# Sparse attention and two expert layers on one core: tiles moved to one offset modulo 512 bytes, scores in quadrants, the last tile's row operations issued later

## Chip, cores and metric

One core of one Trainium2 chip runs the whole program. The metric is the device time of one execution in microseconds (us). The kernel before takes 958.8 us (median of 3 runs, 957.45 to 959.18).

## What is computed

```python
# attention: q, k, v of 4 batches x 8 heads x 576 tokens x 64
scores = (1 / 8) * q @ k.T
scores = where(scores >= max(scores, -1) - tau, scores, -1e9)
attn = exp(scores - max(scores, -1))
attn = attn / (sum(attn, -1) + 1e-9)
x = attn @ v                        # then heads side by side: 2304 x 512
# first expert layer, d_ff 1536
y = ((x @ w_a) * (x @ w_b)) @ w_out
# second expert layer, d_ff 1024
h = y @ w_in
e = exp(h - max(h, -1))
s = h * e / (sum(e, -1) + 1e-9)
ln = (s - mean(s)) / sqrt(var(s) + 1e-6) * g_ln
out = ln @ w_out2
```

All is float32. In the expert layers each operand is split into a high part (rounded to fp32r) and the remainder, and a product is three matmuls: high x high, high x low, low x high.

## The kernel before

The work is issued in the order in which the code stands; each engine takes its instructions in that order.

**Attention** (`attention`) works on 16 pairs of heads (`i`). A pair has nine score tiles `s`: for each of four chunks of 128 tokens one per head, and a ninth, the tail, that holds the last 64 tokens of both heads. The loop over `m` takes two score tiles per step, so nine steps are two pairs. For a tile, `scores` (L281 to L289) multiplies queries by keys on TensorE. The 64-long inner dimension stands twice in the partitions: the lower 64 partitions (`g` = 0) multiply the first half of the keys, the upper 64 (`g` = 1) the second half, into two PSUM banks of one `ps` tile. A float32 matmul of the program runs in two passes and stands twice in the trace, with two weight loads. For a normal tile the products are of 64 rows by 128 columns of the array, for the tail of 64 by 64, with one head in each half of the columns. Then VectorE scales and takes the row minimum (L293, `ns`), ScalarE takes the exponential (L305, `pe`), GpSimd works out the threshold (L310), VectorE masks (L319). A step later TensorE transposes `pe` (L339, and L355, L358 for tails), ScalarE copies it to SBUF (L332), and two steps later TensorE multiplies with `v` (L370). `finish` transposes the reciprocals of a pair (L391, `rt`), ScalarE copies them (L396, `zt`), and a DMA stores them. `rt`, `tp` and `tq` share three PSUM buffers. `PROG` sets the order within a step.

**Weights** arrive as float64 bits; `conv_load` brings 512 columns at a time (`wraw`), and `conv_ops` makes float32 of them (L127 ACT, L131, L134, L137 DVE) and splits them (L141 ACT, L144 POOL). The results go to nine slots of 12288 bytes, five in pool `wp` (w1 groups with `f % 9 < 5`: w1_0 to w1_4 and w1_9 to w1_11, later w2_0 and w2_1) and four in pool `wp2` (w1_5 to w1_8, w2_2 to w2_5).

**First expert layer** (`moe1`): 12 groups `f` of 128 hidden columns, 5 blocks `j` of tokens, four of 512 columns and one of 256 (the tails of all batches). In a first pass every block goes through groups 0 to 5, in a second through 6 to 11. `ab` (L549) makes 24 matmuls, weights `w1_f` loaded and input `xt` streamed; ACT and DVE make `a`, `g` and `gt` (L555 to L558); two units later `yacc` (L572) makes 12 matmuls, weights `w1_f` and `gt` streamed.

**Second expert layer** (`moe2`): 18 tiles `t` of 128 tokens. `hid(t)` makes 24 matmuls (L656: `ys` loaded, `w2` streamed) and then issues the row operations: maximum (L660), exponential (L663), product (L664), mean (L666), centring (L667, `e`), sum of squares (L668), scale (L670 to L677). `lnt(t)` transposes `e` (L689, `pl`), multiplies by `g_ln` (L693, `l`), rounds (L694) and subtracts (L695, on GpSimd, for the last tile on VectorE) to make `lt`. `outp(t)` makes 24 matmuls (L708: `lt` loaded, `w2` streamed), ACT scales the result (L713), a DMA stores it. The loop issues `hid(t)`, `outp(t-2)`, `lnt(t-1)`; at the last tile, 17, `lnt(16)` comes between `hid(17)` and `outp(15)`, and after the loop come half of `outp(16)`, `lnt(17)`, the other half, and `outp(17)`.

Where tiles lie: pools follow each other in SBUF in the order in which they are opened. In the program as built, the pool `const` ends at byte 17184 of a partition, which is 288 modulo 512. The five slots of `wp`, the staging tiles (`wraw`, `w32`, `wlow`) and `xr0`, `zr` stand at 288 modulo 512. Then come the four `vs` tiles of 32 bytes, 128 bytes in all, and everything behind them that the expert layers use (`xt`, the four slots of `wp2`, `gt`, `a32`, `g32`, `ys`, `lt`, `y1`) stands at 416 modulo 512.

Of the kernel before, what the change touches and what calls it, by code (L numbers as in the profile page):

```python
# [8 lines left out]
F32 = mybir.dt.float32  # L9
# [5 lines left out]
ALU = mybir.AluOpType  # L15
AX = mybir.AxisListType
PSUM = bass.MemoryType.PSUM
P = 128
# [3 lines left out]
def kernel(  # L22
# [11 lines left out]
    nc = tc.nc  # L34
    NP, _, VS, D = v.shape
    NQ = VS // 2
    SM = NQ * P
    S = SM + D
    W = S + D
    NT, DM = out.shape  # L40
    B = NT // S
    NPAIR = NP // B
    NF = w1.shape[0]
    KC = DM // P
    DF2 = w_in.shape[2]
    NJ = DF2 // P
    HS = S // 2
# [8 lines left out]
    NTILE = len(TILES)  # L56
# [10 lines left out]
    const = ctx.enter_context(tc.tile_pool(name="const", bufs=1))  # L67
# [17 lines left out]
    xr_p = ctx.enter_context(tc.tile_pool(name="xr", bufs=1))  # L85
# [3 lines left out]
    vs = {}  # L89
# [92 lines left out]
    def load_x(j):  # L182
        n = LEN[j]
        xr = xr_p.tile([P, KC, NB], F32, name="xr0")[:, :, 0:n]
        zr = xr_p.tile([P, KC, NB], F32, name="zr")[:, :, 0:n]
        for b, s0, m, c in BLK[j]:
            nc.sync.dma_start(out=xr[:, :, c:c + m], in_=xd[b][:, :, s0:s0 + m])
            if b not in vs:
                vs[b] = xr_p.tile([P, KC, 2], F32, name="vs", bufs=B)
                nc.sync.dma_start(out=vs[b], in_=xd[b][:, :, S:S + 2])  # L190
                vnew.append(b)
            for h in range(2):
                zs = rzd[b].rearrange("(k h) s -> h k s", h=2)[h:h + 1, :, s0:s0 + m]
                nc.sync.dma_start(out=zr[h * D:(h + 1) * D, :, c:c + m], in_=zs.to_broadcast([D, KC, m]))
        xs[j] = (xr, zr, xhs[j % 2].tile([P, KC, 2, NB], F32R, name="xt")[:, :, :, 0:n])
# [40 lines left out]
    def attention():  # L236
# [43 lines left out]
        def scores(i, s):  # L280
            q, k = ld[i]  # L281
            ps = ps_s.tile([P, 2, 512], F32, name="ps")
            qc, h = divmod(s, 2)
            parts = [(slice(0, P), h, slice(qc * P, (qc + 1) * P), 0)] if s < 2 * NQ else [(slice(u * D, (u + 1) * D), u, slice(SM, S), u * D) for u in range(2)]
            for rows, u, c, o in parts:
                for g in range(2):
                    r = slice(g * D, (g + 1) * D)
                    nc.tensor.matmul(ps[rows, g, 0:HS], lhsT=q[r, u, c], rhs=k[r, u, o:o + HS], start=True, stop=True, skip_group_check=True)  # L288
            st[i, s] = ps  # L289

        def soft_max(i, s, nm):
# [113 lines left out]
        for h in range(2):  # L405
            nc.scalar.dma_start(out=q0[:, h], in_=qkv[0, :, h * (W + D):h * (W + D) + S])
            for g in range(2):
                r, o = slice(g * D, (g + 1) * D), (2 + h) * W + g * HS
# [21 lines left out]
        for m in range(tot // 2 + 6):  # L430
            if m == tot // 2 - 10:
                load_x(0)
# [58 lines left out]
            i, s = divmod(2 * m, NS)  # L491
            r = m - (i * NS + 1) // 2
# [145 lines left out]
    def moe2(ps_t):  # L638
# [5 lines left out]
        def w2(i, u):  # L644
            return w2s[i // 3][:, i % 3, u]

        s1 = {}

        def hid(t):
            y = yt.pop(t)  # L650
            ph = ps_s.tile([P, 2, 512], F32, name="ps")
            for g in range(2):
                k = 0
                for kc in range(KC):
                    for a, b in ((0, 0), (0, 1), (1, 0)):
                        nc.tensor.matmul(ph[:, g, :], lhsT=y[:, a, kc, :], rhs=w2(2 * kc + g, b), start=(k == 0), stop=(k == 3 * KC - 1))  # L656
                        k += 1
            nm = sm.tile([P, 1], F32, name="nm")
            z = sm.tile([P, 3], F32, name="z2")
            nc.vector.tensor_reduce(out=nm, in_=ph, axis=AX.XY, op=ALU.max, negate=True)  # L660
            e = wstage.tile([P, DF2], F32, name="e", tag="wraw", bufs=RB)
            ev = e.rearrange("p (g n) -> p g n", g=2)
            nc.scalar.activation(out=ev, in_=ph, func=AF.Exp, bias=nm, scale=1.0, accum_out=z[:, 0:1])  # L663
            nc.vector.scalar_tensor_tensor(out=ev, in0=ph, scalar=1.0, in1=ev, op0=ALU.mult, op1=ALU.mult, accum_out=z[:, 1:2])  # L664
            mu = sm.tile([P, 1], F32, name="mu")
            nc.vector.tensor_scalar(out=mu, in0=z[:, 1:2], scalar1=1.0 / DF2, scalar2=None, op0=ALU.mult)  # L666
            nc.vector.tensor_scalar(out=e, in0=e, scalar1=mu, scalar2=None, op0=ALU.subtract)  # L667
            nc.scalar.activation(out=ph, in_=ev, func=AF.Square, accum_out=z[:, 2:3])  # L668
            rz = sm.tile([P, 1], F32, name="rz2")
            nc.vector.tensor_scalar(out=rz, in0=z[:, 0:1], scalar1=1e-9, scalar2=None, op0=ALU.add)  # L670
            nc.vector.reciprocal(out=rz, in_=rz)
            t1 = sm.tile([P, 1], F32, name="t1")
            nc.vector.scalar_tensor_tensor(out=t1, in0=z[:, 2:3], scalar=rz, in1=rz, op0=ALU.mult, op1=ALU.mult)
            nc.vector.tensor_scalar(out=t1, in0=t1, scalar1=1.0 / DF2, scalar2=1e-6, op0=ALU.mult, op1=ALU.add)
            t2 = sm.tile([P, 1], F32, name="t2")
            nc.gpsimd.tensor_tensor(out=t2, in0=t1, in1=mhalf, op=ALU.pow)
            nc.gpsimd.tensor_tensor(out=t2, in0=t2, in1=rz, op=ALU.mult)  # L677
            s1[t] = (e, t2)
# [3 lines left out]
        def lnt(t):  # L682
            c, rs = s1.pop(t)
            lt = xh_p.tile([P, 2, NJ, P], F32R, name="lt", tag="xt") if t % 2 else hp.tile([P, 2, NJ, P], F32R, name="lt", bufs=1)
            for g in range(2):
                pl = ps_t.tile([P, NJ // 2, P], F32, name="pl", tag="tp")
                for u in range(NJ // 2):
                    j = g * NJ // 2 + u
                    nc.tensor.transpose(pl[:, u, :], c[:, j * P:(j + 1) * P], ident)  # L689
                gj = slice(g * NJ // 2, (g + 1) * NJ // 2)  # L690
                gb = gl[:, gj].unsqueeze(2).to_broadcast([P, NJ // 2, P])
                l32 = wstage.tile([P, NJ // 2, P], F32, name="l32", tag="w32")
                nc.vector.tensor_tensor(out=l32, in0=pl, in1=gb, op=ALU.mult)  # L693
                nc.scalar.activation(out=lt[:, 0, gj], in_=l32, func=AF.Copy)  # L694
                (nc.vector if t == NTILE - 1 else nc.gpsimd).tensor_tensor(out=lt[:, 1, gj], in0=l32, in1=lt[:, 0, gj].bitcast(F32), op=ALU.subtract)  # L695
            s2[t] = (lt, rs)

        pos = {}
# [22 lines left out]
        for t in range(NTILE):  # L721
            if t + 2 < NTILE:
                load_y(t + 2, yp)
            if t + 1 < NTILE:
                split_y(t + 1, yp)
            hid(t)
            if t == NTILE - 1:
                lnt(t - 1)
            if 0 <= t - 2:
                outp(t - 2)  # L730
            if 0 <= t - 1 < NTILE - 2:
                lnt(t - 1)
# [76 lines left out]
```

## Time and profile before

| | us |
|---|---|
| median of 3 runs (lowest, highest) | 958.8 (957.45, 959.18) |
| profiled execution | 959.81 |
| its span, first to last instruction | 958.0 |
| PE busy | 938.0 (98%) |
| DVE busy | 542.0 (57%) |
| ACT busy | 441.3 (46%) |
| POOL busy | 196.3 (20%) |
| mean granted clock of TensorE | 0.994 |

The span is divided roughly so: attention to 277.7, first expert layer to 732.3, second to the end. A busy time is the union of an engine's instructions; matmuls overlap at their ends, so "busy" divided by their number is the time that each adds.

### The profile page before, as it was taken

What the parts mean: (1) busy time and instruction counts of PE and PEld (TensorE: products, weight loads), DVE (VectorE), ACT (ScalarE), POOL (GpSimd) and SP (SyncE); (2) the same over time, 40 slices, a digit from 0 to 9 for tenths busy, and PEclk for the clock granted to TensorE, in tenths of its full rate; (3) what the DMA queues carried; (4) which work ended last, traced back from release to release, by engine and by line L of the source; (5) the groups of instructions that cost most, each with busy time, mean ns of one, the idle gap of its engine ahead of it and who ended that gap; (6) DMA issues with size and microseconds to landing.
All of it is one profiled execution on the core that took longest, in us unless ns stands there. A gap on an engine that the chain in (4) does not pass through costs nothing.

```text
span 958.0 us, 14042 instructions
## 1 busy us (share of the span) xinstructions
PE 938.0 (98%) x5168; PEld 719.2 (75%) x5168; DVE 542.0 (57%) x1165; ACT 441.3 (46%) x793; POOL 196.3 (20%) x294
## 2 busy tenths in 40 slices
PE   7999999999999999999999999999999999999997
PEld 4656565665667888889888888889988788888885
DVE  6898989889975763223246762222265544444442
ACT  5788887888853451213225532111232433333332
POOL 1112221212221220000013420000022433333331
PEclk9999999999999999999999999999999999999999
DMA  6343343447245563133115541022062111111100
GB/s 176 120 127 112 122 140 102 120 128 199 71 136 154 182 205 75 61 94 132 45 44 199 182 169 67 24 87 78 11 198 66 34 45 44 44 45 44 44 23 34
DMA packets 52612, 95.39 MB, mean 100 GB/s; under 512 B 12736, under 2 KB 28736, under 8 KB 49984
## 3 DMA queue, kind: packets, MB, share of 16 engines
q1 hardware_dynamic: 52112, 93.91, 31.4%
q8 instruction: 41, 0.67, 0.3%
q10 hardware_dynamic: 432, 0.59, 0.2%
q14 instruction: 27, 0.22, 0.1%
HBM read 70.80 MB, written 23.68 MB: 99 GB/s over the span
## 4 chain that ended last, share of the span: by engine, by line
PE 66%; DVE 2%; DMA 2%; ACT 1%; POOL 0%; issue 0%; SPq 0%; ACTq 0%; DVEq 0%
PE ps L549 29%; PE py L572 15%; PE po L708 10%; PE ps L656 9%; PE pl L689 2%; DMA wraw<-in_w_dram 1%; DMA rzd<-zt 0%; POOL lt L695 0%; DVE e L664 0%; ACT e L663 0%; DVE nm L660 0%; ACT ps L668 0%; DVE g L556 0%; DVE e L667 0%; DVE l L693 0%
## 5 line engine op out<-in xcount | busy, mean ns | idle before, releaser
L549 PE MATMUL ps<-xt,w 128*128 128x512 f32 (+1 forms) x1440 | 311.6, 372 | 2.0 <-DVE g L556 2.0
L549 PEld LDWEIGHTS ps<-xt,w 128*128 128x128 f32 x1440 | 253.0, 189 | 51.9 <-DVE g L556 2.4
L144 POOL TENSOR_TENSOR w<-w,w 128x512 fp32r<-128x512 f32 x52 | 77.9, 1497 | 420.2 <-ACT w L141 420.2
L572 PE MATMUL py<-gt,w 128*128 128x512 f32 (+1 forms) x720 | 159.8, 371 | 0.0
L572 PEld LDWEIGHTS py<-gt,w 128*128 128x128 f32 x720 | 126.5, 188 | 24.7
L556 DVE TENSOR_TENSOR g<-ps,a 128x512 f32<-128x512 f32 (+1 forms) x60 | 38.2, 637 | 188.1 <-ACT a L555 188.1
L555 ACT ACTIVATE a<-ps 128x512 f32<-128x512 f32 (+1 forms) x60 | 33.2, 553 | 186.6 <-PE ps L549 183.4
L305 ACT ACTIVATE pe<-ns,nm 128x576 f32<-128x576 f32 x128 | 93.9, 774 | 48.3 <-DVE ns L293 48.1
L319 DVE SCALAR_TENSOR_TENSOR pe<-ns,th,pe 128x576 f32<-128x576 f32 x128 | 102.7, 815 | 16.3 <-ACT pe L305 12.5
L293 DVE TENSOR_SCALAR_CACHE_REDUCE ns<-ps 128x576 f32<-128x576 f32 x144 | 102.6, 749 | 10.7 <-PE ps L288 10.4
L708 PE MATMUL po<-w,lt 128*128 128x512 f32 x432 | 103.6, 395 | 2.7 <-ACT lt L694 1.4
L656 PE MATMUL ps<-w,ys 128*128 128x512 f32 x432 | 104.6, 397 | 1.5 <-POOL ys L524 1.4
L288 PE MATMUL ps<-k,q 64*128 64x288 f32 (+1 forms) x640 | 96.2, 439 | 5.0 <-DMA k<-in_qkv_dram 5.0
L708 PEld LDWEIGHTS po<-w,lt 128*128 128x128 f32 x432 | 81.7, 190 | 21.7 <-ACT lt L694 2.2
L656 PEld LDWEIGHTS ps<-w,ys 128*128 128x128 f32 x432 | 80.0, 188 | 19.6 <-POOL ys L524 1.8
L332 ACT ACTIVATE pt<-tp 128x512 f32<-128x512 f32 (+1 forms) x160 | 78.1, 545 | 1.7 <-PE tp L339 1.4
L310 POOL TENSOR_SCALAR th<-nm,toff 128x1 f32<-128x1 f32 x144 | 38.4, 268 | 188.0 <-DVE ns L293 188.0
L370 PE MATMUL po<-pt,vr 128*64 128x322 f32 (+1 forms) x512 | 76.6, 420 | 0.0
L339 PEld LDWEIGHTS tp<-ident,pe 128*128 128x128 f32 x512 | 56.4, 143 | 26.5 <-issue 14.4
L339 PE MATMUL tp<-ident,pe 128*128 128x128 f32 x512 | 71.6, 280 | 3.3 <-ACT pt L332 2.8
L288 PEld LDWEIGHTS ps<-k,q 64*128 64x128 f32 (+1 forms) x640 | 48.2, 178 | 30.2 <-issue 9.5
L660 DVE TENSOR_REDUCE nm<-ps 128x1 f32<-128x1024 f32 x18 | 22.0, 1224 | 70.0 <-PE ps L656 70.0
(72 smaller groups left out, 820.7 us busy)
## 6 DMA issues: line engine op xcount, KB each, us to landing
wraw<-in_w_dram SPq DMA_DIRECT2D x36, 512.0 KB
q<-in_qkv_dram SPq DMA_DIRECT2D x15, 576.0 KB
k<-in_qkv_dram SPq DMA_DIRECT2D x30, 176.0 KB
xd<-xp SPq DMA_DIRECT2D x16, 289.0 KB
y<-yd SPq DMA_DIRECT2D x18, 256.0 KB
vr<-in_v_dram SPq DMA_DIRECT2D x16, 256.0 KB
xr<-xd SPq DMA_DIRECT2D x4, 1024.0 KB
zr<-rzd SPq DMA_DIRECT2D x8, 512.0 KB
```

What stands on the lines that cost most here:

```text
L144: nc.gpsimd.tensor_tensor(out=w["o"][1], in0=w["f"] if wide else raw, in1=w["o"][0].bitcast(F32), op=ALU.subtract)
L288: nc.tensor.matmul(ps[rows, g, 0:HS], lhsT=q[r, u, c], rhs=k[r, u, o:o + HS], start=True, stop=True, skip_group_check=True)
L293: nc.vector.tensor_scalar(out=ns, in0=st[i, s][:, :, 0:HS], scalar1=-SCALE, scalar2=None, op0=ALU.mult, op1=ALU.min, accum_out=nm)
L305: nc.scalar.activation(out=pe.rearrange("p (g s) -> p g s", g=2), in_=ns, func=AF.Exp, bias=nm, scale=-1.0)
L319: nc.vector.scalar_tensor_tensor(out=pv, in0=ns, scalar=th, in1=pv, op0=ALU.is_le, op1=ALU.mult, accum_out=z[:, s:s + 1])
L332: evac_q.append(lambda: nc.scalar.activation(out=out, in_=in_, func=AF.Copy))
L339: nc.tensor.transpose(tp[:, kc, :], pe[:, o:o + P], ident)
L370: nc.tensor.matmul(po[h * D:(h + 1) * D], lhsT=lhsT, rhs=rhs, start=(kc == 0), stop=(kc == NQ), skip_group_check=True)
L549: nc.tensor.matmul(pa[:, 0:n], lhsT=wt[:, m, wi, kc * P:(kc + 1) * P], rhs=xt[:, kc, xi, :], start=(k == 0), stop=(k == 3 * KC - 1))
L572: nc.tensor.matmul(py, lhsT=wt[:, 2, wi, oc * P:(oc + 1) * P], rhs=gt[:, gi, :], start=(first and k == 0), stop=(last and k == 2))
L656: nc.tensor.matmul(ph[:, g, :], lhsT=y[:, a, kc, :], rhs=w2(2 * kc + g, b), start=(k == 0), stop=(k == 3 * KC - 1))
L708: nc.tensor.matmul(po, lhsT=lt[:, a, j, :], rhs=w2(2 * KC + j, b), start=(k == 0), stop=(k == 3 * NJ - 1))
```

## The change

Three edits, in `load_x`, `scores` and `moe2`.

- `vs`, four tiles of 32 bytes, come from the pool `const` and not from `xr`. `const` then ends at byte 17312, 416 modulo 512. `wp`, the staging tiles, `xr0` and `zr` move up by 128 bytes; everything behind `vs` stays where it was. All large tiles of the expert layers then stand at 416 modulo 512. The tiles of attention don't move.
- In `scores` a normal tile is made of two halves of 64 tokens, each into 64 partitions of `ps`: four products of 64 by 64 of the array in place of two of 64 by 128. The keys that each half streams are the same.
- The row operations of `hid` become a function of their own, `chain`, called after `hid(t)`; at the last tile after `lnt(16)`. The subtraction of `lt` for tile 16 also goes to VectorE.

```diff
@@ load_x
-                vs[b] = xr_p.tile([P, KC, 2], F32, name="vs", bufs=B)
+                vs[b] = const.tile([P, KC, 2], F32, name=f"vs{b}")
@@ scores
-            parts = [(slice(0, P), h, slice(qc * P, (qc + 1) * P), 0)] if s < 2 * NQ else [(slice(u * D, (u + 1) * D), u, slice(SM, S), u * D) for u in range(2)]
-            for rows, u, c, o in parts:
+            parts = [(h, qc * P + u * D, 0) for u in range(2)] if s < 2 * NQ else [(u, SM, u * D) for u in range(2)]
+            for t, (u, c0, o) in enumerate(parts):
+                c = slice(c0, c0 + D)
                 for g in range(2):
                     r = slice(g * D, (g + 1) * D)
-                    nc.tensor.matmul(ps[rows, g, 0:HS], lhsT=q[r, u, c], rhs=k[r, u, o:o + HS], start=True, stop=True, skip_group_check=True)
+                    nc.tensor.matmul(ps[t * D:(t + 1) * D, g, 0:HS], lhsT=q[r, u, c], rhs=k[r, u, o:o + HS], start=True, stop=True, skip_group_check=True)
@@ moe2
+        ph_of = {}
+
         def hid(t):
...
+            ph_of[t] = ph
+
+        def chain(t):
+            ph = ph_of.pop(t)
             nm = sm.tile([P, 1], F32, name="nm")
...
-                (nc.vector if t == NTILE - 1 else nc.gpsimd).tensor_tensor(out=lt[:, 1, gj], in0=l32, in1=lt[:, 0, gj].bitcast(F32), op=ALU.subtract)
+                (nc.vector if t >= NTILE - 2 else nc.gpsimd).tensor_tensor(out=lt[:, 1, gj], in0=l32, in1=lt[:, 0, gj].bitcast(F32), op=ALU.subtract)
...
             hid(t)
             if t == NTILE - 1:
                 lnt(t - 1)
+            chain(t)
             if 0 <= t - 2:
                 outp(t - 2)
```

How TensorE's instructions stand in three steps of attention, the third with a tail tile. `ps` are scores, `tp` transposes, `po` the products with `v`; the shape is output partitions by columns. Before:

```order
L288 MATMUL ps<-k,q 128x288 x4
L339 MATMUL tp<-ident,pe 128x128 x8
L288 MATMUL ps<-k,q 64x288 x4
L288 MATMUL ps<-k,q 128x288 x2
L370 MATMUL po<-pt_129,vr 64x256
```

and with the change:

```order
L289 MATMUL ps<-k,q 64x288 x8
L340 MATMUL tp<-ident,pe 128x128 x8
L289 MATMUL ps<-k,q 64x288 x8
L371 MATMUL po<-pt_129,vr 64x256
L371 MATMUL po<-pt_132,vr 64x256
```

A step of two normal tiles had four matmuls into 128 partitions and has eight into 64; a step with a tail had two shapes and has one.

How VectorE's instructions stand at the end of the second expert layer. `e_8514` belongs to tile 17, `l32_8536` and `l32_8545` to tile 16, `l32_8596` to tile 17. Before:

```order
L660 TENSOR_REDUCE nm_8511<-ps_8486 128x1
L664 SCALAR_TENSOR_TENSOR e_8514,z2_8512<-ps_8486,e_8514 128x1024
L666 TENSOR_SCALAR mu_8517<-z2_8512 128x1
L667 TENSOR_SCALAR e_8514<-e_8514,mu_8517 128x1024
L670 TENSOR_SCALAR rz2_8521<-z2_8512 128x1
L671 RECIPROCAL rz2_8521<-rz2_8521 128x1
L673 SCALAR_TENSOR_TENSOR t1_8524<-z2_8512,rz2_8521 128x1
L674 TENSOR_SCALAR t1_8524<-t1_8524 128x1
L693 TENSOR_TENSOR l32_8536<-pl_8531,gl_91 128x512
L693 TENSOR_TENSOR l32_8545<-pl_8540,gl_91 128x512
L693 TENSOR_TENSOR l32_8596<-pl_8591,gl_91 128x512
L695 TENSOR_TENSOR lt_8590<-l32_8596,lt_8590 128x512
```

and with the change, where `l32_8773` and `l32_8782` belong to tile 16 and `e_8789` to tile 17:

```order
L700 TENSOR_TENSOR l32_8773<-pl_8768,gl_91 128x512
L702 TENSOR_TENSOR lt_8767<-l32_8773,lt_8767 128x512
L700 TENSOR_TENSOR l32_8782<-pl_8777,gl_91 128x512
L702 TENSOR_TENSOR lt_8767<-l32_8782,lt_8767 128x512
L667 TENSOR_REDUCE nm_8786<-ps_8742 128x1
L671 SCALAR_TENSOR_TENSOR e_8789,z2_8787<-ps_8742,e_8789 128x1024
L673 TENSOR_SCALAR mu_8792<-z2_8787 128x1
L674 TENSOR_SCALAR e_8789<-e_8789,mu_8792 128x1024
L677 TENSOR_SCALAR rz2_8796<-z2_8787 128x1
L678 RECIPROCAL rz2_8796<-rz2_8796 128x1
L680 SCALAR_TENSOR_TENSOR t1_8799<-z2_8787,rz2_8796 128x1
L681 TENSOR_SCALAR t1_8799<-t1_8799 128x1
```

Tile 16's two multiplications, and its two subtractions, which GpSimd had, now stand ahead of tile 17's eight row operations. ScalarE's roundings for tile 16 likewise stand ahead of tile 17's exponential.

## Rows read from the trace of the kernel before

**Rows 1.** The page's part 1: busy us (share of the span) and instructions.
```profile
PE 938.0 (98%) x5168; PEld 719.2 (75%) x5168; DVE 542.0 (57%) x1165; ACT 441.3 (46%) x793; POOL 196.3 (20%) x294
```
**Rows 2.** Windows, L549 alone: length, PE busy (x), PEld busy (x), PEclk, DMA, GB/s.
```profile
502.11:526.74 24.63, 16.88 (x72) 13.51 (x72) 1.00 0.55 191
526.74:551.76 25.02, 17.25 (x72) 13.58 (x72) 1.00 0.57 190
```
**Rows 3.** Windows, L572 alone: first with w1_5 to w1_7, then w1_9 to w1_11.
```profile
515.80:534.90 19.10, 8.34 (x36) 6.59 (x36) 1.00 0.75 275
548.90:568.10 19.20, 8.52 (x36) 6.63 (x36) 1.00 0.51 166
```
**Rows 4.** Timeline, PE, second layer: start us, busy us, instruction.
```profile
884.05 5.64 PE L708 MATMUL po<-w,lt 128*128 128x512 f32 x24
...
890.32 5.80 PE L656 MATMUL ps<-w,ys 128*128 128x512 f32 x24
895.96 5.62 PE L708 MATMUL po<-w,lt 128*128 128x512 f32 x24
```
**Rows 5.** Timeline, start of the first layer; in brackets idle time and releaser.
```profile
305.89 0.43 DVE L131 TENSOR_SCALAR wlow<-wraw 128x512 uint32<-128x512 uint32 x1 [7.17 <-DMA wraw<-in_w_dram]
...
307.81 6.47 PE L549 MATMUL ps<-xt,w 128*128 128x512 f32 x20 [1.99 <-DVE g L556]
```
**Rows 6.** Timeline, PE, two steps of attention; the first has a tail tile.
```profile
99.28 1.40 PE L288 MATMUL ps<-k,q 64*128 64x288 f32 x12
100.61 1.08 PE L370 MATMUL po<-pt,vr 128*64 128x256 f32 x8
...
102.65 1.24 PE L288 MATMUL ps<-k,q 64*128 64x288 f32 x8
103.82 1.08 PE L370 MATMUL po<-pt,vr 128*64 128x256 f32 x8
...
106.94 0.44 PE L355 MATMUL tq<-ident,pe 128*128 128x128 f32 x2 [0.52 <-ACT zt L396]
```
**Rows 7.** Groups by line and shape, the scores' weight loads: busy us, mean ns.
```profile
L288 PEld LDWEIGHTS ps<-k,q 64*128 64x128 f32 x512 | 44.9, 189 | 25.8 <-issue 7.3 <-DMA q<-in_qkv_dram 4.4 <-DVE pe L319 2.9
...
L288 PEld LDWEIGHTS ps<-k,q 64*64 64x64 f32 x128 | 3.3, 131 | 4.4 <-issue 2.2 <-DVE pe L319 1.5 <-DVE vs L202 0.4
```
**Rows 8.** Waits from 20 to 260 us: us in total, times, longest.
```profile
DVE ns L293 <- PE ps L288: 6.7, 12, 0.8
```
**Rows 9.** Timeline, DVE, one of these waits.
```profile
108.38 0.76 DVE L293 TENSOR_SCALAR_CACHE_REDUCE ns<-ps 128x576 f32<-128x576 f32 x1 [0.72 <-PE ps L288]
```
**Rows 10.** Timeline, the last two tiles, PE and DVE.
```profile
931.68 1.03 PE L689 MATMUL pl<-ident,e 128*128 128x128 f32 x8
931.88 1.23 DVE L660 TENSOR_REDUCE nm<-ps 128x1 f32<-128x1024 f32 x1 [4.30 <-PE ps L656]
...
932.47 5.71 PE L708 MATMUL po<-w,lt 128*128 128x512 f32 x24
...
935.89 0.76 DVE L667 TENSOR_SCALAR e<-e,mu 128x1024 f32<-128x1024 f32 x1
...
938.12 0.15 DVE L674 TENSOR_SCALAR t<-t 128x1 f32<-128x1 f32 x1
...
939.60 0.73 PE L708 MATMUL po<-w,lt 128*128 128x512 f32 x2 [1.42 <-ACT lt L694]
...
940.96 3.97 PE L708 MATMUL po<-w,lt 128*128 128x512 f32 x10 [0.62 <-POOL lt L695]
...
944.76 1.04 PE L689 MATMUL pl<-ident,e 128*128 128x128 f32 x8
945.47 0.69 DVE L693 TENSOR_TENSOR l<-pl,gl 128x512 f32<-128x512 f32 x1 [5.99 <-PE pl L689]
...
948.85 0.69 DVE L695 TENSOR_TENSOR lt<-l,lt 128x512 fp32r<-128x512 f32 x1 [0.70 <-ACT lt L694]
```
**Rows 11.** Windows, all engines in the tail; the granted clock is the number after POOL.
```profile
940.60:944.00 3.40, 3.04 (x7) 2.46 (x8) 0.00 (x0) 0.12 (x1) 1.54 (x2) 0.50 0.23 82
```

## The prediction

> **What bounds the kernel now.** I read the page's busy times first, then each stage by windows and timelines. TensorE (PE) is busy 938.0 of 958.0 us [rows 1], so a change pays only where it shortens a matmul that PE is really held by, or removes one of PE's few gaps. A busy share does not say which: a matmul can be slow and still "busy". So the second view is the busy time of equal numbers of matmuls, in stretches that differ in their operands alone [rows 2, 3]. The third is the three places where PE waits for others: inside attention [rows 6, 8, 9], at the start of the first expert layer [rows 5], and at the last token tile [rows 10, 11].
>
> **Operands at one offset.** Moving four 32-byte tiles into the first pool shifts five weight slots and the staging tiles from byte 288 to byte 416 modulo 512; the inputs, `gt`, `ys`, `lt` and the four other weight slots stand at 416 already. So the kernel before holds both cases. In block 0's second pass, 72 matmuls with w1_6 to w1_8 (slots at 416) keep PE busy 16.88 us, 72 with w1_9 to w1_11 (slots at 288) 17.25 us [rows 2]: 0.37 us / 72 = 5.1 ns each. The same for the output matmuls, 36 at 8.34 us and 36 at 8.52 us [rows 3]: 5.0 ns. In the second layer the 24 matmuls of `hid` (moving operand `w2`, mostly at 288) take 5.80 us, the 24 of `outp` (all at 416) 5.62 us [rows 4]. But `hid` follows transposes, and an `outp` that follows transposes takes 5.71 us [rows 10], so 0.09 of the 0.18 us is that; the rest is 3.8 ns each.
>
> What is at 288: 8 of 12 weight groups in four blocks of 512 columns. That is 8 x 4 x 24 = 768 matmuls at L549 (3.9 us), 384 at L572 (1.9 us), and 18 x 24 = 432 in `hid` (1.6 us): 7.4 us. I take nothing for the block of 256 columns. Two pieces are lost. The first 120 matmuls run before PE waits 1.99 us for a `g` that stands behind a weight conversion on VectorE (DVE), which waits for a DMA [rows 5]; that wait does not move with PE, so it grows by what they save, 0.6 us. One `hid` at the start of the second layer is followed by such a wait too, 0.1 us. Left: **6.7 us**. PE has no other wait there to hide it, so the bounds are 0 (it isn't the offset, below) and 7.4.
>
> Here a rule speaks against the row. The Trainium skill ("SBUF — State Buffer", section "Who interferes with whom") gives PE two read ports, independent for moving operand and weight load, and says that only the port pair of VectorE and GpSimd causes contention. By it an address could not matter, this part would be worth 0, and the sum below would be 5.0. Rows 2 and 3 differ from it: same shapes, same clock, 5 ns. I go by the rows.
>
> **Scores in quadrants.** Each score tile was two products of 64 rows by 128 columns, each in two passes, so a step of two tiles is four groups of two simultaneous matmuls. Now it is four groups of four quadrants. A step of eight such matmuls takes 103.82 - 102.65 = 1.17 us; a step in which one tile is the 64-token tail, already in quadrants, has also four groups, and takes 100.61 - 99.28 = 1.33 us [rows 6]. Quadrants one after the other would have cost two groups more, so the four do run together; the 0.16 us more I read as the switch between shapes. All in quadrants, that switch goes, and the first weight load of a step, which nothing covers, is of 64 columns: 131 ns for 189 [rows 7], some 0.05 us. In nine steps (two pairs of heads) seven save 0.05 and two 0.21, together 0.77 us; eight times that is 6.2 us of PE time, the upper bound. The lower bound is a loss of 0.5 us, if 512 more matmuls and loads delay the queue by 1 ns each.
>
> The end of attention does not follow PE alone. VectorE waits for scores only 12 times and 6.7 us in 240 us [rows 8]; otherwise it is the chain. Seven of the waits are of 0.72 us like the one at 108.38 [rows 9], in the step after a pair's reciprocals are transposed. There PE itself was held, its transposes waiting for ScalarE's (ACT's) copy of `zt` [rows 6], which stands behind exponentials that wait for VectorE. So these shrink by the 0.05 us only: 7 x 0.05 = 0.35. The other five hold 6.7 - 7 x 0.72 = 1.7 us. PE's lead takes them whole, except the largest, 0.8 us [rows 8], at step 8: VectorE paces the first steps, and from step 4 on PE can have gained some 0.21 + 4 x 0.05 = 0.4. That makes 1.3 us. VectorE thus ends attention **1.6 us** earlier, and since the DMA that the later wait hangs on [rows 5] is issued behind VectorE's conversions, this passes through.
>
> **The last tile.** Before, VectorE gets `hid(17)`'s row operations (first 931.88) ahead of tile 16's `l`; PE ends `outp(15)` near 938.1, waits 1.42 us, runs two matmuls, waits 0.62, and runs ten in 3.97 us, not 2.3, since the granted clock is 0.50 (1.2 GHz) after these waits [rows 10, 11]. The transposes of tile 17 start at 944.76.
>
> After, `l` of tile 16 comes first. By tile 17's rows, `l` starts 945.47 - 944.76 = 0.71 us after the transposes begin, and the second subtraction, on VectorE, ends 948.85 + 0.69 - 945.47 = 4.07 us later. From 931.68 that gives 932.39 and 936.46, before PE needs `lt` at 938.1. So both waits go, and with them the cause of the lower clock. Late next is tile 17's `e`: its chain starts at 936.46, not 931.88, and `e` is centred 935.89 + 0.76 - 931.88 = 4.77 us later, at 941.2. PE has done twelve matmuls (half of 895.96 - 890.32 = 5.64 us [rows 4], so 2.8) by 940.9 and waits 0.3 to 0.4. Transposes at 941.3, not 944.76: **3.4 us**. What follows is as before, for VectorE ends the chain 938.12 + 0.15 - 931.88 = 6.4 us after its start, at 942.9, and `lt` of tile 17 is complete about 4 us later, while `outp(16)` and the first half of `outp(17)` hold PE until 947.7. If the lower clock is not always there, the gain is the two waits less 0.4: 1.6 us. GpSimd loses two subtractions, which nothing else awaits.
>
> **Sum.** 6.7 + 1.6 + 3.4 = 11.7 us. The profiled execution took 959.8 us, 1.0 above the median of 958.8. From its time 948.1; I take it off the median: **947.1 us**. A difference under 0.2% (1.9 us) can't be told from none.
>
> **Rivals.** A: it is not the offset but where the slots lie. All slow slots are the five low ones, so rows 2 and 3 can't part the two; for the offset speaks that `lt` lies in a low and in a high buffer by turns, and two `outp` in a row take 5.64 and 5.62 us [rows 4]. Then 1.6 + 3.4 = 5.0: 953.8. The page's rule gives the same. Chance 0.11.
>
> B, slower: the two column halves of a group now stream the same columns of `k` at once, where the tail's quadrants stream columns of different heads. If two reads of one address exclude each other, a group takes two streams, 2 x 0.24 us (240 ns is the 1.17 us less a lead-in of some 0.2, over four), a tile 0.48 us more, 128 tiles 61 us, all on PE's path: 1010 us. It decides from 10.1 us / 128 = 79 ns a tile upward. Against it: the row above, where operands at like offsets read faster. Chance 0.05.
>
> C: the last tile gives nothing, since tile 17's chain behind `l` keeps PE waiting about as long as before. It would need `e` 3.4 us later than worked out. 958.8 - 8.3 = 950.5. Chance 0.07.
>
> D: attention follows PE after all, and the 6.2 us come whole: 942.5. Chance 0.05.
>
> The forecast keeps 0.72, its own range 943.5 to 950.5 (offset 5.5 to 7.4, attention 0.4 to 4, tail 1.6 to 3.6, and 1 us of spread). The range 943.0 to 952.0 takes in C and the nearer part of A and leaves out B, D and the rest of A, under 2 in 10. Faster by over 0.2%: forecast, C, D and nearly all of A, 0.91; the same 0.04; slower 0.05.
>
> **What would show it.** L549's matmuls at equal busy time with w1_6 to w1_8 and with w1_9 to w1_11, about 16.9 us for 72, and `hid`'s 24 at 5.7. Steps in attention at 1.12 us whatever the tile; fewer waits of VectorE for `ps`, those of 0.7 still there. The wait near 305 still there, a little longer. In the tail `lt` subtracted on VectorE before the reduction, no wait ahead of `outp(16)`, the clock at 1.0. I am wrong if w1_9 stays at 17.2, if a step of scores takes over 1.3 us, or if PE's new wait for `e` is over 1 us.

## The result and the profile after

The changed kernel takes **945.14 us** (median of 4 runs, 943.92 to 946.82), the kernel before, on the same chip, 958.3 us (4 runs, 957.45 to 959.18). The ratio is 0.9864, with a 95% interval of 0.9842 to 0.9885, so the gain lies between 11.0 and 15.1 us. The forecast was 947.1 us. The same kernel measured again on another chip (the last experiment) gave 947.75 against 956.79 us, a ratio of 0.9891 (0.9864 to 0.9918): 9.0 us, with an interval of 7.8 to 13.0. The gain is thus known to some 2 us, and 11.7 us lies inside both intervals.

The profiled execution took 943.92 us, its span 942.1 us. First the page: busy times, and the costliest groups that answer to those of the prediction (busy us, mean ns; then idle time and what ended it).

```profile
PE 922.5 (98%) x5680; PEld 707.3 (75%) x5680; DVE 542.9 (58%) x1167; ACT 439.9 (47%) x793; POOL 193.1 (20%) x292
...
L550 PE MATMUL ps<-xt,w 128*128 128x512 f32 (+1 forms) x1440 | 305.5, 368 | 1.4 <-DVE g L557 1.4
...
L573 PE MATMUL py<-gt,w 128*128 128x512 f32 (+1 forms) x720 | 157.3, 368 | 0.0
...
L659 PE MATMUL ps<-w,ys 128*128 128x512 f32 x432 | 102.7, 393 | 1.6 <-POOL ys L525 1.4
```

PE is busy 15.5 us less than in [rows 1] and still 98% of the span: the matmuls themselves became shorter, while their number grew by 512. A part of it is two stretches in which the kernel before ran matmuls at 1.2 GHz and this execution did not, near 309 us and in the tail [rows 11].

Windows, L550 alone, block 0's second pass, first w1_6 to w1_8, then w1_9 to w1_11, as in [rows 2]:

```profile
494.56:519.04 24.48, 16.81 (x72) 13.51 (x72) 1.00 0.56 190
519.04:543.52 24.48, 16.81 (x72) 13.51 (x72) 1.00 0.58 190
```

The difference of 0.37 us between the two kinds of slots is gone.

Timeline of attention, PE; the last two rows are a score step and what follows it. The row above them, at 105.75, answers to the last one of [rows 6]; the waits below, from 20 to 260 us, to [rows 8].

```profile
105.75 0.44 PE L356 MATMUL tq<-ident,pe 128*128 128x128 f32 x2 [0.87 <-ACT zt L397]
...
262.06 1.20 PE L289 MATMUL ps<-k,q 64*64 64x288 f32 x16
263.19 1.08 PE L371 MATMUL po<-pt,vr 128*64 128x256 f32 x8
```

```profile
DVE ns L294 <- PE ps L289: 5.5, 8, 0.7
```

A score step takes 263.19 - 262.06 = 1.13 us, where it took 1.17 or, with a tail, 1.33 [rows 6]. VectorE waits for scores eight times and not twelve, but the seven waits of 0.7 us remain, and PE still waits for `zt`, 0.87 us here.

Timeline of the first layer's start (SPq is SyncE's queue), against [rows 5]:

```profile
288.86 0.57 SPq L187 DMA_DIRECT2D xr<-xd  x1
...
290.15 1.38 SPq L194 DMA_DIRECT2D zr<-rzd  x2
291.64 3.60 SPq L112 DMA_DIRECT2D wraw<-in_w_dram  x2
...
303.28 0.43 DVE L131 TENSOR_SCALAR wlow<-wraw 128x512 uint32<-128x512 uint32 x1 [6.75 <-DMA wraw<-in_w_dram]
...
305.21 5.75 PE L550 MATMUL ps<-xt,w 128*128 128x512 f32 x24 [1.45 <-DVE g L557]
```

In the kernel before, the 24 matmuls behind the wait:

```profile
307.81 7.40 PE L549 MATMUL ps<-xt,w 128*128 128x512 f32 x24 [1.99 <-DVE g L556]
```

The weights that VectorE waits for are issued behind the loads of `xr` and `zr` for block 1. PE's wait is 1.45 us and was 1.99. Before, the 24 matmuls behind the wait took 7.40 us, not 5.75, and the granted clock was 0.50 (1.2 GHz) from 309.1 to 312.5; here it stayed at 1.00.

Timeline of the last two tiles, PE and VectorE, against [rows 10]:

```profile
919.22 1.03 PE L696 MATMUL pl<-ident,e 128*128 128x128 f32 x8
919.93 0.69 DVE L700 TENSOR_TENSOR l<-pl,gl 128x512 f32<-128x512 f32 x1 [4.69 <-PE pl L696]
...
920.01 8.42 PE L715 MATMUL po<-w,lt 128*128 128x512 f32 x36
...
923.31 0.69 DVE L702 TENSOR_TENSOR lt<-l,lt 128x512 fp32r<-128x512 f32 x1 [0.70 <-ACT lt L701]
923.92 1.22 DVE L667 TENSOR_REDUCE nm<-ps 128x1 f32<-128x1024 f32 x1
...
927.92 0.75 DVE L674 TENSOR_SCALAR e<-e,mu 128x1024 f32<-128x1024 f32 x1
...
928.82 1.06 PE L696 MATMUL pl<-ident,e 128*128 128x128 f32 x8 [0.39 <-DVE rz L677]
```

`outp(15)` and half of `outp(16)` run as one row of 36 without a wait; the only wait left is 0.39 us for `e` of tile 17.

**Where the 15.9 us between the two profiled executions went.** Up to the end of PE's wait near 305: 307.81 - 305.21 = 2.60 us. From there to the first `hid` (732.33 and 721.88): 424.52 - 416.67 = 7.85, of which some 1.6 is the missing stretch at 1.2 GHz. From the first `hid` to the last one (926.02 and 913.67): 193.69 - 191.79 = 1.90. From there to the end: 32.0 - 28.4 = 3.6. The profiled execution before (959.81 us) was slower than all four runs of its kernel, and the one after (943.92) the fastest of its four, so 15.9 us is more than the gain.

### The profile page after: what moved, and what is told of

The parts are those of the page before. It is cut to its first block, busy times and chain, and to the rows that moved or that the text cites. A ratio compares the mean times of both kernels' runs of the same rounds, so it can differ in the third digit from the quotient of the medians.

```text
span 942.1 us, 15066 instructions
## 1 busy us (share of the span) xinstructions
PE 922.5 (98%) x5680; PEld 707.3 (75%) x5680; DVE 542.9 (58%) x1167; ACT 439.9 (47%) x793; POOL 193.1 (20%) x292
## 4 chain that ended last, share of the span: by engine, by line
PE 65%; DVE 2%; DMA 2%; ACT 1%; SPq 0%; issue 0%; POOL 0%; ACTq 0%; DVEq 0%
PE ps L550 29%; PE py L573 15%; PE po L715 10%; PE ps L659 9%; PE pl L696 2%; DMA wraw<-in_w_dram 1%; DVE e L671 0%; ACT e L670 0%; DVE nm L667 0%; DMA rzd<-zt 0%; ACT ps L675 0%; DVE e L674 0%; DVE l L700 0%; ACT lt L701 0%; DVE g L557 0%
## 5 line engine op out<-in xcount | busy, mean ns | idle before, releaser
L550 PE MATMUL ps<-xt,w 128*128 128x512 f32 (+1 forms) x1440 | 305.5, 368 | 1.4 <-DVE g L557 1.4
L550 PEld LDWEIGHTS ps<-xt,w 128*128 128x128 f32 x1440 | 251.5, 189 | 46.8 <-DVE g L557 1.9
L573 PE MATMUL py<-gt,w 128*128 128x512 f32 (+1 forms) x720 | 157.3, 368 | 0.0
L573 PEld LDWEIGHTS py<-gt,w 128*128 128x128 f32 x720 | 126.3, 189 | 22.5
L320 DVE SCALAR_TENSOR_TENSOR pe<-ns,th,pe 128x576 f32<-128x576 f32 x128 | 102.7, 815 | 16.4 <-ACT pe L306 12.5
L294 DVE TENSOR_SCALAR_CACHE_REDUCE ns<-ps 128x576 f32<-128x576 f32 x144 | 102.6, 749 | 8.6 <-PE ps L289 8.6
L659 PE MATMUL ps<-w,ys 128*128 128x512 f32 x432 | 102.7, 393 | 1.6 <-POOL ys L525 1.4
L715 PE MATMUL po<-w,lt 128*128 128x512 f32 x432 | 101.4, 390 | 0.7 <-POOL lt L702 0.6
L289 PE MATMUL ps<-k,q 64*64 64x288 f32 x1152 | 90.7, 424 | 4.9 <-DMA k<-in_qkv_dram 4.9
L659 PEld LDWEIGHTS ps<-w,ys 128*128 128x128 f32 x432 | 79.8, 188 | 18.1 <-POOL ys L525 1.8
L371 PE MATMUL po<-pt,vr 128*64 128x322 f32 (+1 forms) x512 | 79.2, 427 | 0.1
L371 PEld LDWEIGHTS po<-pt,vr 128*64 128x64 f32 x512 | 34.6, 138 | 39.6 <-issue 16.8
L289 PEld LDWEIGHTS ps<-k,q 64*64 64x64 f32 x1152 | 37.4, 134 | 31.9 <-issue 7.8
```

The costliest lines, as they stand in the source:

```text
L289: nc.tensor.matmul(ps[t * D:(t + 1) * D, g, 0:HS], lhsT=q[r, u, c], rhs=k[r, u, o:o + HS], start=True, stop=True, skip_group_check=True)
L294: nc.vector.tensor_scalar(out=ns, in0=st[i, s][:, :, 0:HS], scalar1=-SCALE, scalar2=None, op0=ALU.mult, op1=ALU.min, accum_out=nm)
L320: nc.vector.scalar_tensor_tensor(out=pv, in0=ns, scalar=th, in1=pv, op0=ALU.is_le, op1=ALU.mult, accum_out=z[:, s:s + 1])
L371: nc.tensor.matmul(po[h * D:(h + 1) * D], lhsT=lhsT, rhs=rhs, start=(kc == 0), stop=(kc == NQ), skip_group_check=True)
L550: nc.tensor.matmul(pa[:, 0:n], lhsT=wt[:, m, wi, kc * P:(kc + 1) * P], rhs=xt[:, kc, xi, :], start=(k == 0), stop=(k == 3 * KC - 1))
L573: nc.tensor.matmul(py, lhsT=wt[:, 2, wi, oc * P:(oc + 1) * P], rhs=gt[:, gi, :], start=(first and k == 0), stop=(last and k == 2))
```

## The experiments

In this table are places of the profiled executions, in us from the start of the span. `zt` is ScalarE's last copy of attention; "released" is PE's start after the first layer's wait, and "waited" that wait.

| kernel | `zt` | released | waited | first `hid` | `hid(17)` | end |
|---|---|---|---|---|---|---|
| before | 283.44 | 307.81 | 1.99 | 732.33 | 926.02 | 958.0 |
| after | 281.24 | 305.21 | 1.45 | 721.88 | 913.67 | 942.1 |
| offset alone | 282.91 | 307.35 | 1.90 | 725.60 | 917.41 | 949.4 |
| quadrants alone | 281.61 | 307.82 | 4.38 | 733.31 | 927.00 | 957.6 |
| last tile alone | 282.67 | 306.87 | 2.44 | 731.44 | 925.10 | 953.6 |
| reciprocals later | 277.63 | 301.06 | 1.15 | 717.71 | 909.51 | 938.0 |
| loads split | 277.91 | 300.00 | none | 716.52 | 908.70 | 937.1 |
| without quadrants | 282.87 | 306.83 | 1.42 | 724.46 | 916.27 | 944.7 |
| after, again | 280.99 | 305.69 | 2.40 | 728.35 | 920.16 | 948.6 |

### The offset alone

```diff
-                vs[b] = xr_p.tile([P, KC, 2], F32, name="vs", bufs=B)
+                vs[b] = const.tile([P, KC, 2], F32, name=f"vs{b}")
```

> The kernel before with one edit: the four vs tiles come from const, so that all large tiles of the expert layers stand at 416 modulo 512. Theory (unequal offsets of loaded weights and streamed operand cost 5 ns a matmul): 72 matmuls of the first layer keep PE busy 16.8 to 16.9 us with any weight group, hid and outp 5.6 to 5.7 us per tile, and the run is 6 to 8 us faster than before (951 to 952). Rival (the gain in the first layer came from attention handing over sooner, or from clock drops): under 3 us, 955.5 or more.

Measured: 949.41 us (4 runs, 946.74 to 951.2) against 957.8 (19 runs, 955.69 to 962.68), ratio 0.9904 (0.9867 to 0.9941): 8.4 us, with an interval of 5.7 to 12.7. Groups by line and shape, with the offset:

```profile
L549 PE MATMUL ps<-xt,w 128*128 128x512 f32 x1152 | 270.6, 391 | 1.9 <-DVE g L556 1.9
...
L572 PE MATMUL py<-gt,w 128*128 128x512 f32 x576 | 138.1, 389 | 0.0
...
L656 PE MATMUL ps<-w,ys 128*128 128x512 f32 x432 | 102.6, 393 | 1.6 <-POOL ys L524 1.4 <-ACT ys L523 0.2
...
L549 PE MATMUL ps<-xt,w 128*128 128x256 f32 x288 | 36.5, 283 | 0.0
```

and before:

```profile
L549 PE MATMUL ps<-xt,w 128*128 128x512 f32 x1152 | 275.3, 395 | 2.0 <-DVE g L556 2.0
...
L572 PE MATMUL py<-gt,w 128*128 128x512 f32 x576 | 140.6, 393 | 0.0
...
L656 PE MATMUL ps<-w,ys 128*128 128x512 f32 x432 | 104.6, 397 | 1.5 <-POOL ys L524 1.4
```

The matmuls of 256 columns were busy 36.3 us before, and both executions have one stretch at 1.2 GHz behind the wait. So 4.7 + 2.5 + 2.0 = 9.2 us come off the matmuls of 512 columns, and none off those of 256. Of these, by the table, (424.52 - 418.25) + (193.69 - 191.81) = 8.15 us lie behind the wait.

### The quadrants alone

```diff
-            parts = [(slice(0, P), h, slice(qc * P, (qc + 1) * P), 0)] if s < 2 * NQ else ...
+            parts = [(h, qc * P + u * D, 0) for u in range(2)] if s < 2 * NQ else ...
...
```

> The kernel before with one edit: scores in quadrants. Theory (PE gains some 6 us in attention, VectorE's chain passes 1.5 to 2.5 us of it on): the first matmul of the first layer 1.4 us earlier, VectorE's later wait for g 2 to 2.6 us earlier, and 956 us, 1.5 to 3 us faster than before. Rival (PE's gain passes whole): 952. Rival (none passes): 958.

Measured: 958.36 us (10 runs, 954.44 to 962.8), ratio 0.9996 (0.9972 to 1.0019): no gain is seen, though the interval, from 1.8 us lost to 2.7 gained, has room for the 1.6 us of the forecast. Timeline at the first layer's start, and a window behind the wait (all engines; granted clock after POOL):

```profile
305.90 0.43 DVE L131 TENSOR_SCALAR wlow<-wraw 128x512 uint32<-128x512 uint32 x1 [8.99 <-DMA wraw<-in_w_dram]
...
307.82 8.37 PE L550 MATMUL ps<-xt,w 128*128 128x512 f32 x24 [4.38 <-DVE g L557]
```

```profile
306.60:313.20 6.60, 5.38 (x13) 4.22 (x14) 4.72 (x8) 3.22 (x5) 0.00 (x0) 0.50 0.05 20
```

Attention did end earlier: the last `zt` by 1.83 us, and the load of `xr` for block 1 was issued 1.83 us earlier too (289.23 against 291.06 us). But in this execution these loads took longer: the weights behind them were issued 0.96 us earlier (293.00 against 293.96) and were there at the same time as before. So PE waited 4.38 us, and then ran at 1.2 GHz for twice as long as in the kernel before. In this execution the gain was taken back here in full.

### The last tile alone

```diff
...
+            ph_of[t] = ph
+
+        def chain(t):
+            ph = ph_of.pop(t)
...
-                (nc.vector if t == NTILE - 1 else nc.gpsimd).tensor_tensor(out=lt[:, 1, gj], ...
+                (nc.vector if t >= NTILE - 2 else nc.gpsimd).tensor_tensor(out=lt[:, 1, gj], ...
...
                 lnt(t - 1)
+            chain(t)
```

> The kernel before with the last edits alone: chain after lnt(16), and the subtraction of tile 16 on VectorE. Theory: from the transposes of tile 16 to those of tile 17 9.6 us in place of 13.1, no clock drop in between, 955 us, 3 to 3.6 us faster. Rival (before, the clock drop is there in few executions): 1.6 to 2.2 us faster in the median.

Measured: 956.22 us (10 runs, 953.47 to 959.9), ratio 0.9982 (0.9963 to 1.0001): 1.6 us, with an interval from 0.1 us lost to 3.5 gained, at the edge of what the runs can tell. In the profiled execution the tail is as worked out:

```profile
930.76 1.03 PE L695 MATMUL pl<-ident,e 128*128 128x128 f32 x8
931.55 8.43 PE L714 MATMUL po<-w,lt 128*128 128x512 f32 x36
940.36 1.06 PE L695 MATMUL pl<-ident,e 128*128 128x128 f32 x8 [0.38 <-DVE rz L676]
```

From one tile's transposes to the next it takes 9.60 us. With the old tail it was 13.08 in [rows 10] and 13.22 with the offset alone, but 11.67 with the quadrants alone: there the two waits of 1.42 and 0.62 us stand too, and the ten matmuls behind them take 2.56 us, without a fall of the clock. So the tail gives 3.5 us where the clock had fallen and 2.1 where it had not. Which of the two is commoner isn't known from three profiles. The runs lean to the second: 1.6 us is what the rival in the expectation said for a fall in few executions, and the mean granted clock is 0.9972 over these ten runs and 0.9968 over the 19 before, where 3.4 us at half the clock in every run would make a difference of 0.0018. That is a hint, since the mean also moves with falls elsewhere.

### The high slots moved by 128 bytes more

This is the changed kernel with one added tile at the start of `wp2`. It moves `wp2`'s four slots and all behind them to 32 modulo 512, and leaves the lower ones at 416.

```diff
         pools[False] = wp2
+        nc.gpsimd.memset(wp2.tile([P, 32], F32, name="pad", bufs=1), 0.0)
```

> The changed kernel with a tile of 128 bytes ahead of the four weight slots of the second pool: these four and all that lies behind them (the second xt, gt, ys, lt of even tiles, y1) move to 32 modulo 512, the five other slots, the first xt and lt of odd tiles stay at 416. Theory (what counts is whether loaded and streamed operand stand alike): outp of even tiles (32 and 32) takes 5.45 us from start to the next start as in the changed kernel, outp of odd tiles (32 and 416) 0.1 us longer; w1_6 to w1_8 take 16.3 us per 72 matmuls in the blocks whose xt is at 32 and 16.7 where it is at 416, w1_9 to w1_11 the other way round; in all 6 to 8 us more than the changed kernel. Rival (byte 416 is good and any other place bad): both kinds of outp are slow. Rival (the place of the slots counts, not the offset): no difference from the changed kernel.

Measured, one run: 951.0 us. PE's busy time at L550, L573 and L659 is 308.8, 159.8 and 104.6 us, and 305.5, 157.3 and 102.7 after: the last two have their values of the kernel before again (159.8 and 104.6), and the first is half way back to 311.6, with the same slots in the same order. Timeline, second layer:

```profile
902.22 5.74 PE L715 MATMUL po<-w,lt 128*128 128x512 f32 x24
...
908.59 5.81 PE L659 MATMUL ps<-w,ys 128*128 128x512 f32 x24
914.24 5.62 PE L715 MATMUL po<-w,lt 128*128 128x512 f32 x24
```

`outp` is slow and fast by turns, as `lt` lies in its low buffer (416) and in its high one (32), while `w2` is at 32 here. A mean over all such matmuls of the trace gives 232.5 ns from one start to the next with `lt` at 416 and 227.4 with `lt` at 32. For `ab` it is 228.0 with both at 32, 227.5 with both at 416, and 233.2 and 232.8 for the two unequal pairs. So neither the value of the offset nor the slot counts, only whether the loaded and the streamed operand agree.

### Moved by 256 bytes, and by 32

```diff
+        nc.gpsimd.memset(wp2.tile([P, 64], F32, name="pad", bufs=1), 0.0)
```

> As e4_shift_high with a tile of 256 bytes: the four high slots, the second xt, gt, ys and lt of even tiles stand at 160 modulo 512, the others at 416. Theory (any unequal place modulo 512 costs some 5 ns a matmul): outp of odd tiles 0.1 us longer than that of even tiles, w1_9 to w1_11 with gt at another place 16.7 us per 72 matmuls. Rival (the places only have to agree modulo 256): all as fast as in the changed kernel, 944 to 947.

```diff
+        nc.gpsimd.memset(wp2.tile([P, 8], F32, name="pad", bufs=1), 0.0)
```

> As e4_shift_high with a tile of 32 bytes: 448 against 416. Theory (any unequal place costs some 5 ns a matmul): outp of odd tiles 0.1 us longer than that of even tiles, 950 to 954 in all. Rival (a small distance costs less, for the two reads part at once): under half of that.

Measured, one run each: 945.56 us with 256 bytes, 951.67 with 32. Timelines of the second layer, first 256 bytes:

```profile
885.52 5.61 PE L715 MATMUL po<-w,lt 128*128 128x512 f32 x24
...
891.75 5.71 PE L659 MATMUL ps<-w,ys 128*128 128x512 f32 x24
897.30 5.61 PE L715 MATMUL po<-w,lt 128*128 128x512 f32 x24
```

and 32 bytes:

```profile
891.00 5.60 PE L715 MATMUL po<-w,lt 128*128 128x512 f32 x24
...
897.23 5.83 PE L659 MATMUL ps<-w,ys 128*128 128x512 f32 x24
902.90 5.76 PE L715 MATMUL po<-w,lt 128*128 128x512 f32 x24
```

With operands 256 bytes apart all matmuls are as fast as with equal offsets (5.61 and 5.61; 5.71); 32 bytes apart they are as slow as 128 apart. As far as these distances tell, what has to agree is the place modulo 256, not 512.

### The reciprocals transposed a step later

This is the changed kernel, with `finish` of every second pair called one step later, which puts `rt` behind the score tiles.

```diff
-                        if m - j * NS // 2 == 9:
+                        if m - j * NS // 2 == 10 - j % 2:
                             finish(j)
```

> The changed kernel; the transposes of the reciprocals of even pairs one step later, where no tq needs their PSUM buffer. Theory (seven times VectorE waits 0.7 us for scores because PE stands at tq until ScalarE has copied zt): these seven waits of VectorE shrink to under 0.3, attention ends 2 to 4.5 us earlier, 941 to 943.5. Rival (VectorE and ScalarE are full, the wait only moves to another place): attention ends within 0.5 us of the changed kernel's, 944 to 947.

Measured: 940.69 us (4 runs, 939.73 to 942.58) against 956.7 (7 runs, 954.97 to 959.9), ratio 0.9836 (0.9808 to 0.9864). Waits from 20 to 258 us, and PE's timeline at the step shown of after:

```profile
DVE ns L294 <- PE ps L289: 2.1, 4, 0.6
```

```profile
104.35 0.38 PE L356 MATMUL tq<-ident,pe 128*128 128x128 f32 x2
...
104.93 1.20 PE L289 MATMUL ps<-k,q 64*64 64x288 f32 x16
106.06 0.28 PE L392 MATMUL rt<-ident,rz 128*9 128x128 f32 x1
```

The transposes no longer stand behind `zt`, and VectorE's waits shrink from 5.5 to 2.1 us. Attention ends 281.24 - 277.63 = 3.6 us earlier, and this time the whole program does: its span is 4.1 us shorter, and the four runs (939.73 to 942.58 us) lie below all ten of the changed kernel (943.92 to 950.38), though not all on one chip.

It was expected that all seven waits of 0.7 us would shrink to under 0.3, and four of them did. They are gone: those behind the places at which PE waits for `zt` in the profile after (0.87, 0.34, 0.76 and 0.87 us). At the other three PE shows no wait for `zt`, and there VectorE still waits, twice for 0.41 us and once for 0.64:

```profile
41.59 0.76 DVE L294 TENSOR_SCALAR_CACHE_REDUCE ns<-ps 128x576 f32<-128x576 f32 x1 [0.64 <-PE ps L289]
```

This shows what held four of the seven; what holds the rest stays open.

### Block 1's loads one unit later, and split

First the changed kernel with the load of block 1 (`xr`, `zr`) issued one unit later, and its conversions too:

```diff
-            prep = n < n1 and f in (2, 3)
+            prep = n < n1 and f in (3, 4)
...
-                if n == 0:
+                if n == 1:
                     load_x(1)
...
-                        prep_x(j + 1, f - 2)
+                        prep_x(j + 1, f - 3)
                 elif prep:
-                    prep_x2(0, 2 * f - 4)
+                    prep_x2(0, 2 * f - 6)
```

> The changed kernel; the load of block 1's inputs one unit later, and their preparation one unit later too, so that the weights come ahead of them in the DMA queue. Theory (the wait for g near 305 is for weights that stand behind these inputs in the queue): no wait over 0.5 us before unit 4, no clock drop there, 1.5 to 4 us faster in the median, 941 to 943.5, and runs that differ less. Rival (the queue is full anyway and the next weights or the inputs come late instead): a wait of 1 us or more a few units later, 944 to 947.

Measured: 943.16 us (4 runs, 941.83 to 946.41), ratio 0.986 (0.9832 to 0.9889), not to be told from the change. The wait moved and stayed:

```profile
303.03 5.60 PE L550 MATMUL ps<-xt,w 128*128 128x512 f32 x24
...
311.39 0.43 DVE L131 TENSOR_SCALAR wlow<-wraw 128x512 uint32<-128x512 uint32 x1 [7.48 <-DMA wraw<-in_w_dram]
...
313.31 6.87 PE L550 MATMUL ps<-xt,w 128*128 128x512 f32 x22 [1.96 <-DVE g L557]
```

The weights of unit 4 now come in time and those of unit 5, which stand behind the loads instead, come late. So I split them: the reciprocals later as above, `xr` in unit 0, `zr` in unit 1, and the conversions one unit later.

```diff
-    def load_x(j):
+    def load_x(j, parts="xz"):
...
-                if n == 0:
-                    load_x(1)
+                if n < 2:
+                    load_x(1, "xz"[n])
...
```

> e7_finish_later, and the load of block 1 in two parts, xr one unit before zr, prepared one unit later. Theory (a weight load comes late because 2 MB stand ahead of it in one piece): with 1 MB ahead of each weight load VectorE's longest wait for wraw near 300 falls from 6 to 7 us to under 4, PE doesn't wait before unit 6, and the run is 1 to 3 us faster than e7_finish_later, 938 to 940. Rival (the queue is full there): PE waits 1 us or more at another unit, 940 to 941.

Measured: **938.85 us** (4 runs, 938.47 to 940.1) against 956.79 (11 runs, 955.66 to 962.08), ratio 0.9798 (0.9769 to 0.9828). It beats both kernels. PE runs through the first layer's start without a wait:

```profile
300.00 5.60 PE L554 MATMUL ps<-xt,w 128*128 128x512 f32 x24
...
308.16 5.60 PE L554 MATMUL ps<-xt,w 128*128 128x512 f32 x24
```

Against the reciprocals alone (0.9836) the intervals overlap, so the split's own gain isn't shown by the times; that the wait is gone is.

### The change without quadrants, and the change again

The edit of the first is the quadrants' undone, on the changed kernel; the second is the changed kernel as it is.

> The changed kernel with the scores as before (64 rows by 128 columns). Theory (quadrants bring what VectorE's chain passes on): 1.5 to 2.5 us slower than e11_changed in the median, and VectorE's subtraction of block 0's inputs starts 1.5 to 2 us later in the trace. Rival (the later wait for weights takes it back): within 0.5 us of e11_changed.

> The changed kernel once more, for e10_no_quadrants on the same chip: 944 to 947.

Measured: without quadrants 946.62 us (6 runs, 945.5 to 947.67), ratio 0.9876 (0.9849 to 0.9903); with them 947.75 (6 runs, 945.75 to 950.38), ratio 0.9891 (0.9864 to 0.9918). The quadrants bring no gain that the times show: on this chip 1.6 us would have put the median with them at 945.0 us, below all six of its runs. That is neither the 1.5 to 2.5 us expected nor the rival's 0.5 at most. `zt` is 282.87 without and 280.99 with them, so the 1.9 us are there at the end of attention, and 1.1 us of them at PE's release (306.83 and 305.69); they were lost after it. The profile with them is that of the slowest of the six runs (950.38 us). Timelines of the change again, ScalarE and PE, and the window (all engines; granted clock after POOL):

```profile
343.95 0.67 ACT L127 ACTIVATE w<-wraw 128x512 f32<-128x512 f32 x1 [7.22 <-DMA wraw<-in_w_dram]
...
346.40 2.04 ACT L577 ACTIVATE y<-py 128x512 f32<-128x512 f32 x4
...
347.04 5.49 PE L573 MATMUL py<-gt,w 128*128 128x512 f32 x12 [2.97 <-ACT y L577]
```

```profile
346.00:350.00 4.00, 2.96 (x7) 2.38 (x8) 2.85 (x5) 3.53 (x7) 0.96 (x1) 0.51 0.41 135
```

A second group of weights is late here. ScalarE's conversion waits for it with the evacuation of `y` queued behind, PE waits 2.97 us for that, and its next twelve matmuls take 5.49 us, not 2.88, at half the clock. The same wait was 1.52 us with 256 bytes, 0.65 without quadrants and with the later load, and absent in the profile of after.

## Why the prediction was right

**The offset: right in kind, too small.** The step "left: 6.7 us" is the term that was mis-sized: 8.15 us behind the wait. Two sizes in it failed. I took a matmul at equal offsets in the kernel before as the case without the cost; but some of these ran behind matmuls at unequal offsets, and 72 of them went from 16.88 [rows 2] to 16.81 us as well: in the kernel before, the first seven of the 24 at 502.11, behind output matmuls at unequal offsets, follow each other by 224 to 236 ns, and the 24 at 518.58, behind matmuls at equal offsets, by 226 or 227. So a matmul at unequal offsets lost more: for 72 of them 17.25 - 16.81 = 0.44 us, which is 6.1 ns each and not 5.1. For `hid` I took 3.8 ns for 432 matmuls; its group lost 104.6 - 102.6 = 2.0 us, not 1.6. That blocks of 256 columns give nothing held.

Rival A fell. The lower slots became fast by 128 bytes, and the higher ones slow by another 128. The Trainium skill ("SBUF — State Buffer", "Who interferes with whom"), which makes PE's two reads independent and by which this part was worth nothing, differs from what was measured, and the measurement decides: 232.5 against 227.4 ns for the same shape and clock, with the high slots moved. What joins the two reads in the chip isn't shown by any run.

**Scores in quadrants: the mechanism right in the main, its passage to the end wrong.** A step took 1.13 us (1.12 worked out), and attention ended 1.6 us earlier by the working and 1.83 and 1.88 us by the two pairs of profiles that differ in this alone. The last `zt` lies at 282.7 to 283.4 us in the four profiles without quadrants, and at 280.7 to 281.6 in the seven with them that leave `finish` in its place. VectorE's waits for scores shrank by 6.7 - 5.5 = 1.2 us; no run shows where the other half microsecond comes from. One reading was wrong, though the sum did not suffer, for these waits stayed at 0.70 us: I put all seven waits of 0.7 us down to `zt`, from one row. PE shows a wait for `zt` at only three of the seven places in the kernel before and at four after, and the later reciprocals removed just these four.

The step that failed is "this passes through". The lead did reach PE's release near 305 in five of the six profiles that have quadrants, with `finish` and the loads in their places: it lies at 303.7 to 305.7 us, and at 306.8 to 307.8 without quadrants. But with quadrants alone the late weights were there at 305.9 us as before, and the lead became a longer wait; and to the end of the program it came in neither comparison of times. Whether the quadrants bring on the later wait near 346 or it only fell so in these executions stays open. Rival B fell: a step with shared keys is not slower. Rival D fell: attention's end moved by some 2 us and not by 6.2.

**The wait near 305.** I said that it would be a little longer; it was 1.45 us in the profile, less than before, and 2.40 when the change was measured again. VectorE's start on these weights, counted from the last `zt`, lies between 21.1 and 24.3 us in the profiles whose loads stand as in the change, and that moves the wait by more than my 0.6 us. That the wait hangs on the DMA behind block 1's loads is shown by the two experiments that moved these: it moved with them, and with the loads apart it was gone. These two waits, and the clock that falls behind them in some executions, lie where the executions differ; I took this spread as 1 us, and the kernel before alone has 955.69 to 962.68 us.

**The last tile: the path right, its worth in the time less sure.** `l` came 0.71 us after the transposes, the second subtraction ended 923.31 + 0.69 - 919.93 = 4.07 us later, the centring 927.92 + 0.75 - 923.92 = 4.75 (4.77 worked out), and PE's new wait was 0.39 us (0.3 to 0.4). From transposes to transposes it went from 13.08 to 9.60 us: 3.5 against 3.4. The clock stayed at 1.00. The case "if the lower clock is not always there" (1.6 us) came up as well, with 2.1 us, and the times of this edit alone, 1.6 us, lie nearer to it than to 3.4. Rival C fell by these rows; the times alone could not have told it from the forecast.

**The sum.** 11.7 us was forecast; the two measurements gave 13.2 and 9.0. The larger offset term and the lost quadrants nearly cancel: 8.15 + 3.5 = 11.7 again. That is luck, not the working: two errors of 1.5 and 1.6 us with opposite signs, and a tail of 3.5 us that the times do not confirm. The times of the three edits alone add up to 8.4 - 0.6 + 1.6 = 9.4 us.

## What to carry to other kernels

Compare equal matmuls that differ only in where their operands lie: an engine that is 98% busy can still have about one per cent in the addresses (8 of 958 us here), and a pad of some bytes is a cheap trial. A lead that one stage gains is worth nothing where the next waits for a transfer that does not start earlier; follow the queue in which that transfer is issued before the gain is booked. Where a wait can bring the clock down, removing it pays for itself and for the slow matmuls behind it, but only in those executions in which the clock fell.

## What was not expected of the hardware

- A matmul of 512 columns (float32 rounded to fp32r) whose loaded and streamed operand stand 32 or 128 bytes apart modulo 512 takes 232 to 233 ns from start to start; with 0 or 256 bytes between them it takes 227 to 228.
- Four quadrants of the array ran together also where two of them streamed the same columns: 16 such matmuls in 1.13 us.
- After PE waits of 1.5 to 4.4 us the granted clock fell to 0.50 (1.2 GHz) in some executions and in others not: not after 1.45 us and 2.40 us in the changed kernel's first wait, but after 1.90 us with the offset alone and 2.44 us with the last tile alone, for 3.4 us each, and after 4.38 and 2.97 us for nearly 7.
